# Attention values with v as the stationary operand, and softmax sums spread by a matrix of ones

## The chip, the cores and the metric

The kernel runs on one core of one Trainium2 chip. The metric is the device time of one execution in microseconds (us), lower is better. The profile is of one execution; its engines are PE (TensorE matmuls), PEld (TensorE weight loads), DVE (VectorE), ACT (ScalarE), POOL (GpSimd) and SP (SyncE, here a queue of DMAs).

## What is computed

Eight batches of eight heads, 576 tokens and 64 elements a head. Heads 0 to 3 see a sliding window of 32 tokens, heads 4 to 7 a dilated window: every fourth token, 32 of them. The result goes through a two-layer network with a squared ReLU.

```python
# q, k, v: (8, 8, 576, 64) float32; w_in (512, 2048); w_out (2048, 512)
scores = q @ k.T / sqrt(64)
rel = pos[:, None] - pos[None, :]
mask_plain = (rel >= 0) & (rel < 32)                    # heads 0..3
mask_dil = (rel >= 0) & (rel < 128) & (rel % 4 == 0)    # heads 4..7
attn = softmax(where(mask, scores, -1e9))
x = (attn @ v).transpose(0, 2, 1, 3).reshape(4608, 512)
out = maximum(x @ w_in, 0) ** 2 @ w_out                 # (4608, 512) float32
```

## The kernel before

The order of instructions on each engine is the order in which the program writes them (a manual schedule). Every batch has an attention part; its 576 result rows go, transposed, into `xT` (512 features over 4 x 128 partitions, all 4608 tokens). The network runs over nine chunks of 512 tokens: `mm1_gen` makes 16 tiles `ph` of 128 hidden features by 512 tokens (four matmuls each), ScalarE takes the ReLU (`rt`, L269) and VectorE its square (`g`, L270); `mm2_gen` makes four tiles `po` of 128 tokens by 512 outputs (16 matmuls each), ScalarE copies them out (`ot`, L284) and a DMA stores them (L285, on SP's queue but for chunk 0).

The two are interleaved by hand. A generator yields after every two matmuls of the network, and `pump(n)` issues the next n of these steps, so a step is two 512-column matmuls. A chunk has 64 steps, 32 of `mm1` and 32 of `mm2`; the stores of its four token tiles fall in steps 40, 48, 56 and 64. In the loop over batches 2 to 7, the chunk `b - 1` runs beside batch `b`: 24 steps, then the scores with a gap of 4 steps behind each of four groups, then the values with a gap of 2 behind each of eleven but the last, then what is left. Batch 1 runs beside the second half of chunk 0 (`mm2_by_rows_gen`) with gaps of 1 and 2. Batch 0 has no network work yet; there `fill_gen` puts idle matmuls (`pf`) between its groups.

Attention in a batch, by groups on TensorE:

- Batches 0 and 1 are transposed on TensorE (`t_sliding` into `pt`, `t_dilated` into `pd`, copies by VectorE and ScalarE); later ones come through a DRAM tile and a transposing DMA (`keep_sliding_qk`, `keep_dilated_qk`, `transpose_sliding`, `transpose_dilated`). `after_transposes` makes GpSimd wait for these before it issues the next loads. GpSimd also reorders q and k (`by_token`, `nr`) and casts v (`cast_v`).
- Scores: `s_sliding` (12 matmuls `ps` of 96 columns) and `s_dilated` (16 matmuls `pz` of 72 columns), two of each. They contract over 64 elements, so two heads' matmuls stand in the two halves of the rows. A result tile has keys on the partitions and queries along the free axis. `softmax` takes the exponential on ScalarE (L380) and the product with a 0/1 mask on VectorE (L381) and leaves the weights in `AT`.
- Values: `av_sliding` (three groups `pav`) and `av_dilated` (four groups `paw`). Each has eight matmuls with a 128x128 piece of the weights as the stationary operand and v, with a 65th column of ones, as the moving one. The 65th column of the result is the sum of the weights. `normalize` takes its reciprocal (L423) and multiplies (L424) into `x`, with tokens on the partitions.
- Transposes: `x_sliding` and `x_dilated` turn `x` round (`px`, `py`, two groups each), and ScalarE copies it into `xT` (L473, L491).

The attention groups take their PSUM from `papool`, which has two buffers of two banks, so a group waits until the tile two before it has been read. The network's tiles have four banks of their own (`pmool`).

Of the kernel before, what the change touches and what calls it, by code (L numbers as in the profile page):

```python
# [13 lines left out]
P = 128  # L14
# [3 lines left out]
def kernel(  # L18
# [13 lines left out]
    DIL = 4  # L32
# [27 lines left out]
    xp = ctx.enter_context(tc.tile_pool(name="xp", bufs=4))  # L60
# [19 lines left out]
    AT = const.tile([P, 8, 640], FP16, name="AT")  # L80
    vp = [const.tile([P, NB, HH, D + 2], FP16, name=f"vp{r}") for r in range(2)]
    vd = [const.tile([P, 2, DIL, HH, D + 2], FP16, name=f"vd{r}") for r in range(2)]
# [3 lines left out]
    maskp = const.tile([P, UW], FP16, name="maskp")  # L86
    maskd = const.tile([P, UW], FP16, name="maskd")
# [70 lines left out]
    def cast_sliding_v(b):  # L158
        for m in range(0, NB, 2):
            nc.gpsimd.tensor_copy(vp[b % 2][:, m : m + 2, :, 0:D], sv[:, m : m + 2, :, :])  # L160

    def cast_dilated_v(b):
        for t in range(2):
            for c in range(0, DIL, 2):
                nc.gpsimd.tensor_copy(  # L165
                    vd[b % 2][:, t, c : c + 2, :, 0:D],
                    sd[:, t, :, D * c : D * (c + 2)].rearrange("p h (c d) -> p c h d", d=D),
                )
# [44 lines left out]
    warm = const.tile([P, 1], FP32, name="warm")  # L213
    nc.vector.memset(warm, 0.0)
    nc.scalar.activation(warm, warm, ACTF.Exp)
# [17 lines left out]
    nc.vector.memset(AT[:, :, UW:640], 0.0)  # L233
    for r in range(2):
        nc.vector.memset(QKTp[r][:, 1, :, 0:PADP], 0.0)
        nc.vector.memset(QKTd[r][:, 1, :, 0:KPAD], 0.0)
        nc.vector.memset(vp[r][:, :, :, D : D + 1], 1.0)
        nc.vector.memset(vp[r][0:PADP, 0, :, D : D + 1], 0.0)
        nc.vector.memset(vd[r][:, 1, :, :, D : D + 1], 1.0)
        nc.vector.tensor_scalar(  # L240
            out=vd[r][:, 0, :, :, D],
            in0=relf[:, 0:1].unsqueeze(2).to_broadcast([P, DIL, HH]),
            scalar1=-PADD + 0.5,
            scalar2=None,
            op0=ALU.is_lt,
        )
# [118 lines left out]
    def t_dilated(b, n, a, wide):  # L365
        for w, (s0, s1) in enumerate(((0, 5), (5, 9))):
            p_ = pt(f"pd{b}_{a}_{w}", wide)
            for s in range(s0, s1):
                j = 4 * s + 2 * a
                nc.tensor.transpose(  # L370
                    p_[:, P * (s - s0) : P * (s - s0 + 1)], n[:, D * j : D * (j + 2)], ident
                )
            copy(
                nc.scalar if w else nc.vector,
                QKTd[b % 2][:, :, a, KPAD:].rearrange("x i (c s) -> x i c s", s=9)[:, :, :, s0:s1],
                p_[:, 0 : P * (s1 - s0)].rearrange("x (s i c) -> x i c s", i=2, c=64),
            )

    def softmax(u, ps, mask):
        nc.scalar.activation(AT[:, u, 0:UW], ps[:, :, 0 : UW // 2], ACTF.Exp, scale=scale)  # L380
        nc.vector.tensor_mul(AT[:, u, 0:UW], AT[:, u, 0:UW], mask)  # L381

    def s_sliding(b, hp):
        tiles = [pa(f"ps{b}_{hp}_{half}") for half in range(2)]
        for half, ps in enumerate(tiles):
            for m3 in range(3):
                m = 3 * half + m3
                for e in range(2):
                    r = slice(D * e, D * (e + 1))
                    nc.tensor.matmul(  # L390
                        ps[:, e, QB * m3 : QB * (m3 + 1)],
                        QKTp[b % 2][r, 1, hp, QB * m : QB * m + P],
                        QKTp[b % 2][r, 0, hp, PADP + QB * m : PADP + QB * (m + 1)],
                        start=True,
                        stop=True,
                    )
        for half, ps in enumerate(tiles):
            softmax(2 * hp + half, ps, maskp)
# [20 lines left out]
    def normalize(b, what, pav, w):  # L419
        x = xp.tile([QB, 2, HH, D], FP16, name=f"x{b}_{what}", tag="x")  # L420
        rcp = xp.tile([QB, 2, HH], FP32, name=f"rcp{b}_{what}", tag="rcp")
        pv = pav[0:w, :, 0 : HH * (D + 2)].rearrange("p i (h d) -> p i h d", d=D + 2)
        nc.vector.reciprocal(rcp[0:w], pv[:, :, :, D])  # L423
        nc.vector.tensor_tensor(  # L424
            out=x[0:w],
            in0=pv[:, :, :, 0:D],
            in1=rcp[0:w].unsqueeze(3).to_broadcast([w, 2, HH, D]),
            op=ALU.mult,
        )
        return x  # L430

    def av_sliding(b, mp):
        pav = pa(f"pav{b}_{mp}")
        for i in range(2):
            m = 2 * mp + i
            for h in range(HH):
                off = (h % 2) * 288 + (m % 3) * QB
                nc.tensor.matmul(  # L438
                    pav[:, i, h * (D + 2) : h * (D + 2) + D + 1],
                    AT[:, 2 * (h // 2) + m // 3, off : off + P],  # L440
                    vp[b % 2][:, m, h, 0 : D + 1],
                    start=True,
                    stop=True,
                )
        return normalize(b, f"p{mp}", pav, QB)

    def av_dilated(b, t, a):
        pav = pa(f"paw{b}_{t}_{a}")
        for e in range(2):
            for h in range(HH):  # L450
                off = e * 288 + a * 144 + t * QD
                nc.tensor.matmul(  # L452
                    pav[:, e, h * (D + 2) : h * (D + 2) + D + 1],
                    AT[:, 4 + h, off : off + P],
                    vd[b % 2][:, t, 2 * a + e, h, 0 : D + 1],
                    start=True,
                    stop=True,
                )
        return normalize(b, f"d{t}_{a}", pav, QD)

    def x_sliding(b, half, xs, wide):
        px = pt(f"px{b}_{half}", wide)
        for m3 in range(3):
            m = 3 * half + m3
            x = xs[m // 2][:, m % 2].rearrange("p h d -> p (h d)")
            for c in range(2):
                nc.tensor.transpose(  # L467
                    px[:, 288 * c + QB * m3 : 288 * c + QB * (m3 + 1)],
                    x[:, P * c : P * (c + 1)],
                    ident[0:QB, 0:QB],  # L470
                )
        t0 = b * S + 288 * half
        nc.scalar.copy(  # L473
            xT[:, 0:2, t0 : t0 + 288],
            px[:, 0:UW].rearrange("x (c t) -> x c t", c=2),
        )

    def x_dilated(b, t, xs, wide):
        py = pt(f"py{b}_{t}", wide)
        for a in range(2):  # L480
            for e in range(2):
                x = xs[a][:, e].rearrange("p h d -> p (h d)")
                for c in range(2):
                    o = 288 * c + QD * (2 * a + e)
                    nc.tensor.transpose(  # L485
                        py[:, o : o + QD],
                        x[0:QD, P * c : P * (c + 1)],
                        ident[0:QD, 0:QD],
                    )
        t0 = b * S + 288 * t  # L490
        nc.scalar.copy(  # L491
            xT[:, 2:4, t0 : t0 + 288].rearrange("x c (i r) -> x c i r", r=DIL),
            py[:, 0:UW].rearrange("x (c r i) -> x c i r", c=2, r=DIL),
        )

    def attn_scores(b, gap, less=0):
        for hp in range(2):
            s_sliding(b, hp)
            pump(gap)
        for g in range(2):  # L500
            s_dilated(b, g)
            pump(gap - g * less)

    def attn_values(b, gap, wide=False):
        xs = []
        for mp in range(3):
            xs.append(av_sliding(b, mp))
            pump(gap)
        x_sliding(b, 0, xs, wide)
        pump(gap)  # L510
        ys = [av_dilated(b, 0, 0)]
        pump(gap)
        x_sliding(b, 1, xs, wide)
        pump(gap)
        ys.append(av_dilated(b, 0, 1))
        pump(gap)
        zs = []
        for a in range(2):
            zs.append(av_dilated(b, 1, a))
            pump(gap)  # L520
        x_dilated(b, 0, ys, wide)
        pump(gap)
        x_dilated(b, 1, zs, wide)
# [12 lines left out]
    pending.append(fill_gen())  # L536
    for hp in range(2):
        s_sliding(0, hp)
        pump(1)
    for a in range(2):  # L540
        t_dilated(0, m, a, False)
    pump(2)
    for g in range(2):
        s_dilated(0, g)
        pump(1)
    load_w_out((0, 1))
# [11 lines left out]
    attn_values(0, 1)  # L558
# [7 lines left out]
    pump(7)  # L566
    n, m = nsd[1]
    for hp in range(2):
        t_sliding(1, n, hp, True)
        pump(1)  # L570
    for a in range(2):
        t_dilated(1, m, a, True)
        pump(1)
    attn_scores(1, 2, 1)
    attn_values(1, 1, True)
# [7 lines left out]
    for b in range(2, B):  # L583
# [11 lines left out]
        pump(24)  # L595
        attn_scores(b, 4)
        if not last:
            dp = keep_sliding_qk(b + 1, nr)
        attn_values(b, 2)
# [37 lines left out]
```

The softmax here doesn't subtract the row's maximum and nothing guards it: scores larger than these inputs give would overflow.

## Time and profile before

| | us |
|---|---|
| three runs | 321.22, 321.86, 323.31; median 321.86 |
| the profiled execution | 320.36 |
| its span, first to last instruction | 318.3 |
| matmuls po and ph, 576 of 512 columns each | 140.8 and 128.3 busy |
| matmuls paw (256) and pav (192), 65 columns | 13.3 and 10.0 busy |
| matmuls ps (192) and pz (256) | 7.5 and 7.2 busy |
| transposes py (128) and px (96) | 6.9 and 6.7 busy |

Busy time is a union of intervals; the duration of one pipelined matmul (379 ns for 512 columns, 193 ns for 65) is longer than the distance to the next. What a group costs TensorE is therefore read from the starts of its neighbours. In the lists of instruction groups, "out<-in" are tiles by the program's names, L numbers are lines, and the last figures are busy us, the mean ns of one, and the engine's idle time before.

### The profile page before, as it was taken

What the parts mean: (1) busy time and instruction counts of PE and PEld (TensorE: products, weight loads), DVE (VectorE), ACT (ScalarE), POOL (GpSimd) and SP (SyncE); (2) the same over time, 40 slices, a digit from 0 to 9 for tenths busy, and PEclk for the clock granted to TensorE, in tenths of its full rate; (3) what the DMA queues carried; (4) which work ended last, traced back from release to release, by engine and by line L of the source; (5) the groups of instructions that cost most, each with busy time, mean ns of one, the idle gap of its engine ahead of it and who ended that gap; (6) DMA issues with size and microseconds to landing.
All of it is one profiled execution on the core that took longest, in us unless ns stands there. A gap on an engine that the chain in (4) does not pass through costs nothing.

```text
span 318.3 us, 6260 instructions
## 1 busy us (share of the span) xinstructions
PE 302.9 (95%) x2484; PEld 157.8 (50%) x2484; DVE 162.2 (51%) x353; ACT 168.7 (53%) x286; POOL 79.2 (25%) x119
## 2 busy tenths in 40 slices
PE   1899989999999999999999999999999999999995
PEld 1455544454555445545555455555554555445542
DVE  5683548447543674369435952596256525203400
ACT  2726635568436834684368536762577256316611
POOL 4192018403480361137012800371000000000000
PEclk9999999999999999999999999999999999999999
DMA  7999998999999993998399839984810110010011
GB/s 126 197 155 215 207 210 144 195 257 192 211 259 224 205 270 100 217 194 184 106 205 184 191 91 216 191 172 126 173 44 1 68 68 0 27 72 36 1 66 66
DMA packets 79213, 46.67 MB, mean 147 GB/s; under 512 B 54352, under 2 KB 72784, under 8 KB 79184
## 3 DMA queue, kind: packets, MB, share of 16 engines
q1 hardware_dynamic: 64928, 31.60, 40.8%
q0 software_dynamic: 14256, 14.68, 28.1%
q8 instruction: 19, 0.31, 0.4%
q14 instruction: 10, 0.08, 0.1%
HBM read 39.85 MB, written 16.52 MB: 177 GB/s over the span
## 4 chain that ended last, share of the span: by engine, by line
PE 68%; DMA 12%; DVE 7%; SPq 5%; POOL 3%; issue 2%; ACT 2%; POOLq 0%; ACTq 0%
PE ph L259 31%; PE po L274 31%; SPq L120 4%; DMA wi<-in_moe_w_in_dram 4%; DVE AT L381 3%; DMA sd<-in_v_dram 2%; PE paw L452 2%; DMA sv<-in_v_dram 2%; DMA ns<-in_q_dram 2%; DVE g L270 1%; DMA out_dram<-ot 1%; PE ps L390 1%; PE pav L438 1%; DMA QKTp<-dp 1%; PE py L485 1%
## 5 line engine op out<-in xcount | busy, mean ns | idle before, releaser
L274 PE MATMUL po<-wo,g 128*128 128x512 f16 x576 | 140.8, 379 | 0.0
L259 PE MATMUL ph<-xT,wi 128*128 128x512 f16 x576 | 128.3, 380 | 0.3 <-ACT xT L491 0.3
L270 DVE TENSOR_TENSOR g<-rt 128x512 f16<-128x512 f16 x144 | 66.2, 462 | 98.5 <-ACT rt L269 98.0
L269 ACT ACTIVATE rt<-ph 128x512 f16<-128x512 f32 x144 | 85.9, 599 | 31.4 <-PE ph L259 31.0
L259 PEld LDWEIGHTS <-wi 128*128 128x128 f16 x576 | 64.1, 113 | 58.1 <-issue 0.7
L274 PEld LDWEIGHTS <-g 128*128 128x128 f16 x576 | 49.7, 97 | 46.3
L284 ACT COPY ot<-po 128x512 f32<-128x512 f32 x36 | 21.1, 587 | 54.0 <-PE po L274 51.4
L473 ACT COPY xT<-px 128x576 f16<-128x576 f16 x16 | 10.2, 639 | 31.8 <-PE px L467 31.8
L160 POOL CAST vp<-sv 128x512 f16<-128x512 f32 x24 | 16.5, 712 | 32.9 <-DMA sv<-in_v_dram 32.9
L381 DVE TENSOR_TENSOR AT<-AT,maskd 128x576 f16<-128x576 f16 x32 | 20.3, 664 | 5.3 <-ACT AT L380 4.4
L424 DVE TENSOR_TENSOR x_d<-paw,rcp_d 72x512 f16<-72x512 f32 x32 | 22.0, 687 | 1.1
L380 ACT ACTIVATE AT<-pz 128x576 f16<-128x576 f32 x32 | 18.9, 650 | 5.7 <-PE pz L409 5.6
L165 POOL CAST vd<-sd 128x512 f16<-128x512 f32 x32 | 20.9, 691 | 4.2 <-DMA sd<-in_v_dram 3.6
L381 DVE TENSOR_TENSOR AT<-AT,maskp 128x576 f16<-128x576 f16 x32 | 18.0, 568 | 5.1 <-ACT AT L380 2.8
L380 ACT ACTIVATE AT<-ps 128x576 f16<-128x576 f32 x32 | 19.0, 650 | 1.1 <-PE ps L390 1.0
L111 POOL COPY nr<-ns 128x2304 f16<-128x2304 f16 x6 | 13.0, 2161 | 25.6 <-DMA ns<-in_q_dram 25.6
L204 POOL COPY seen<-QKTp 128x1 f16<-128x1 f16 x5 | 1.3, 267 | 63.0 <-DMA QKTp<-dp 63.0
L424 DVE TENSOR_TENSOR x_p<-pav,rcp_p 96x512 f16<-96x512 f32 x24 | 16.5, 687 | 0.8
L423 DVE RECIPROCAL rcp_d<-paw 72x8 f32<-72x8 f32 x32 | 6.5, 202 | 19.5 <-PE paw L452 19.5
L452 PEld LDWEIGHTS <-AT 128*128 128x128 f16 x256 | 12.1, 98 | 8.5 <-PE px L467 1.0
L491 ACT COPY xT<-py 128x576 f16<-128x576 f16 x16 | 10.2, 640 | 10.7 <-PE py L485 10.5
L452 PE MATMUL paw<-vd,AT 128*128 128x65 f16 x256 | 13.3, 193 | 0.1
(58 smaller groups left out, 143.2 us busy)
## 6 DMA issues: line engine op xcount, KB each, us to landing
out_dram<-ot SPq DMA_DIRECT2D x32, 256.0 KB, 2.2
sv<-in_v_dram SPq DMA_DIRECT2D x40, 128.0 KB, 5.3
sd<-in_v_dram SPq DMA_DIRECT2D x8, 512.0 KB, 10.9
dp<-nr SPq DMA_DIRECT2D x12, 288.0 KB, 4.3
ns<-in_k_dram POOLq DMA_DIRECT2D x8, 288.0 KB, 6.0
ns<-in_q_dram POOLq DMA_DIRECT2D x8, 288.0 KB, 7.4
sd<-in_v_dram SPq DMA_DIRECT2D x8, 288.0 KB
wo<-in_moe_w_out_dram POOLq DMA_DIRECT2D x4, 512.0 KB, 12.9
```

The lines of the kernel that those rows point to most:

```text
L111: nc.gpsimd.tensor_copy(r.rearrange("x j h d -> x h j d"), n.rearrange("x h (j d) -> x h j d", d=D))
L160: nc.gpsimd.tensor_copy(vp[b % 2][:, m : m + 2, :, 0:D], sv[:, m : m + 2, :, :])
L165: nc.gpsimd.tensor_copy(vd[b % 2][:, t, c : c + 2, :, 0:D], sd[:, t, :, D * c : D * (c + 2)].rearrange("p h (c d) -> p c h d", d=D),)
L259: nc.tensor.matmul(ph, wi4[ffc // 4][:, dmk, :, ffc % 4], xs[:, dmk, :], start=(dmk == 0), stop=(dmk == NDM - 1),)
L269: nc.scalar.activation(rt, ph[:], ACTF.Relu)
L270: nc.vector.tensor_mul(g[:, ffc, :], rt, rt)
L274: nc.tensor.matmul(po, g[:, ffc, t * P : (t + 1) * P], wo[ffc // 4][:, ffc % 4, :], start=(ffc == 0), stop=(ffc == NFF - 1),)
L284: nc.scalar.copy(ot, po)
L380: nc.scalar.activation(AT[:, u, 0:UW], ps[:, :, 0 : UW // 2], ACTF.Exp, scale=scale)
L381: nc.vector.tensor_mul(AT[:, u, 0:UW], AT[:, u, 0:UW], mask)
L424: nc.vector.tensor_tensor(out=x[0:w], in0=pv[:, :, :, 0:D], in1=rcp[0:w].unsqueeze(3).to_broadcast([w, 2, HH, D]), op=ALU.mult,)
L452: nc.tensor.matmul(pav[:, e, h * (D + 2) : h * (D + 2) + D + 1], AT[:, 4 + h, off : off + P], vd[b % 2][:, t, 2 * a + e, h, 0 : D + 1], st ...
```

## The change

The values are computed transposed. `v` (128 tokens by 64 elements, without the column of ones) is the stationary operand and the masked weights are the moving one, so a matmul gives 64 elements by 96 or 72 queries. Two heads fill the upper and lower half of the partitions of one PSUM tile, in the layout of `xT`; the transposes and their copies go.

The sums come from matmuls of their own: `ones` (128x64) is stationary, the weights move in pieces of 288 columns, and each sum stands in all 64 partitions of its head (`st`). `shares` takes the logarithm of these on ScalarE and the exponential of its negative, which is the inverse (`r`, 128 x 576 float32). VectorE multiplies `u` by `r` into `xT`.

Padded keys, until now kept out of the sums by zeros in the column of ones, are kept out by masks: `maskp0` for the first half of the sliding heads, and zeros in `maskd`. One activation table with both functions is loaded by name. The order changes too: `attn_scores` holds the four `shares` groups between and behind the scores with one gap for all, `attn_values` has four groups in place of eleven, the loop pumps 22, then gaps of 3 and 3, and in batch 0 all copies of `t_dilated` are VectorE's.

```diff
-        nc.vector.reciprocal(rcp[0:w], pv[:, :, :, D])
-        nc.vector.tensor_tensor(
-            out=x[0:w],
-            in0=pv[:, :, :, 0:D],
-            in1=rcp[0:w].unsqueeze(3).to_broadcast([w, 2, HH, D]),
-            op=ALU.mult,
+    HW = UW // 2
+
+    def shares(b, what, weights):
+        st = pa(f"st{b}_{what}")
+        for h in range(HH):
+            e = slice(D * (h % 2), D * (h % 2 + 1))
+            nc.tensor.matmul(st[e, h // 2, 0:HW], ones, weights(h), start=True, stop=True)
+        r = rp.tile([P, 2, HW], FP32, name=f"r{b}_{what}", tag="r")
+        nc.scalar.activation(r, st[:, :, 0:HW], ACTF.Ln)
+        nc.scalar.activation(r, r, ACTF.Exp, scale=-1.0)
+        return r
...
+    def av_sliding(b, half, r):
+        u = pa(f"up{b}_{half}")
+        for m3 in range(3):
             for h in range(HH):
-                off = (h % 2) * 288 + (m % 3) * QB
+                e = slice(D * (h % 2), D * (h % 2 + 1))
+                off = HW * (h % 2) + QB * m3
                 nc.tensor.matmul(
-                    pav[:, i, h * (D + 2) : h * (D + 2) + D + 1],
-                    AT[:, 2 * (h // 2) + m // 3, off : off + P],
-                    vp[b % 2][:, m, h, 0 : D + 1],
+                    u[e, h // 2, QB * m3 : QB * (m3 + 1)],
+                    vp[b % 2][:, 3 * half + m3, h, :],
+                    AT[:, 2 * (h // 2) + half, off : off + QB],
...
+        nc.vector.tensor_mul(xT[:, 0:2, t0 : t0 + HW], u[:, :, 0:HW], r)
+
+    def av_dilated(b, t, r):
+        u = pa(f"ud{b}_{t}")
+        for c in range(DIL):
             for h in range(HH):
...
+                    u[e, h // 2, QD * c : QD * (c + 1)],
+                    vd[b % 2][:, t, c, h, :],
+                    by_class(h, t)[:, c // 2, c % 2],
...
+    def attn_scores(b, gap):
+        rs = []
         for hp in range(2):
             s_sliding(b, hp)
             pump(gap)
+        for half in range(2):
+            rs.append(shares_sliding(b, half))
+            pump(gap)
         for g in range(2):
             s_dilated(b, g)
-            pump(gap - g * less)
...
+        for t in range(2):
+            rs.append(shares_dilated(b, t))
             pump(gap)
+        return rs
+
+    def attn_values(b, rs, gap):
+        for half in range(2):
+            av_sliding(b, half, rs[half])
+            pump(gap)
+        for t in range(2):
+            av_dilated(b, t, rs[2 + t])
+            if t == 0:
+                pump(gap)
...
-    pump(7)
+    pump(4)
     n, m = nsd[1]
     for hp in range(2):
         t_sliding(1, n, hp, True)
-        pump(1)
+        pump(3)
     for a in range(2):
         t_dilated(1, m, a, True)
-        pump(1)
-    attn_scores(1, 2, 1)
-    attn_values(1, 1, True)
+        pump(2)
+    rs = attn_scores(1, 1)
+    pump(2)
+    attn_values(1, rs, 1)
...
-        pump(24)
-        attn_scores(b, 4)
+        pump(22)
+        rs = attn_scores(b, 3)
         if not last:
             dp = keep_sliding_qk(b + 1, nr)
-        attn_values(b, 2)
+        attn_values(b, rs, 3)
```

More of the change, by code (lines that the diff above doesn't have):

```diff
@@ L59 @@
     natp = ctx.enter_context(tc.tile_pool(name="natp", bufs=4))
-    xp = ctx.enter_context(tc.tile_pool(name="xp", bufs=4))
+    rp = ctx.enter_context(tc.tile_pool(name="rp", bufs=4))
     gp = ctx.enter_context(tc.tile_pool(name="gp", bufs=2))
@@ L79 @@
     QKTd = [const.tile([P, 2, 2, KPAD + S], FP16, name=f"QKTd{r}") for r in range(2)]
-    AT = const.tile([P, 8, 640], FP16, name="AT")
-    vp = [const.tile([P, NB, HH, D + 2], FP16, name=f"vp{r}") for r in range(2)]
-    vd = [const.tile([P, 2, DIL, HH, D + 2], FP16, name=f"vd{r}") for r in range(2)]
+    AT = const.tile([P, 8, UW], FP16, name="AT")
+    vp = [const.tile([P, NB, HH, D], FP16, name=f"vp{r}") for r in range(2)]
+    vd = [const.tile([P, 2, DIL, HH, D], FP16, name=f"vd{r}") for r in range(2)]
+    ones = const.tile([P, D], FP16, name="ones")
     sv = stg.tile([P, NB, HH, D], FP32, name="sv")
@@ L86 @@
     maskp = const.tile([P, UW], FP16, name="maskp")
+    maskp0 = const.tile([P, UW], FP16, name="maskp0")
     maskd = const.tile([P, UW], FP16, name="maskd")
@@ L159, in cast_sliding_v @@
         for m in range(0, NB, 2):
-            nc.gpsimd.tensor_copy(vp[b % 2][:, m : m + 2, :, 0:D], sv[:, m : m + 2, :, :])
+            nc.gpsimd.tensor_copy(vp[b % 2][:, m : m + 2], sv[:, m : m + 2, :, :])
     def cast_dilated_v(b):
@@ L165, in cast_dilated_v @@
                 nc.gpsimd.tensor_copy(
-                    vd[b % 2][:, t, c : c + 2, :, 0:D],
+                    vd[b % 2][:, t, c : c + 2],
                     sd[:, t, :, D * c : D * (c + 2)].rearrange("p h (c d) -> p c h d", d=D),
@@ L212 @@
     make_identity(nc, ident)
-    warm = const.tile([P, 1], FP32, name="warm")
-    nc.vector.memset(warm, 0.0)
-    nc.scalar.activation(warm, warm, ACTF.Exp)
+    nc.scalar.preload_act_table_set("natural_log_exp_and_others")
     relf = const.tile([P, QB], FP32, name="relf")
@@ L232 @@
         )
-    nc.vector.memset(AT[:, :, UW:640], 0.0)
+    nc.vector.tensor_copy(maskp0, maskp)
+    nc.vector.memset(maskp0.rearrange("p (e m w) -> p e m w", e=2, m=3)[0:PADP, :, 0], 0.0)
+    nc.vector.memset(maskd.rearrange("p (n t w) -> p n t w", t=2, w=QD)[0:PADD, :, 0], 0.0)
+    nc.vector.memset(ones, 1.0)
     for r in range(2):
@@ L236 @@
         nc.vector.memset(QKTd[r][:, 1, :, 0:KPAD], 0.0)
[L237 to L246, printed above, removed]
     wi4 = []
@@ L363, in t_sliding, with t_dilated @@
             )
-    def t_dilated(b, n, a, wide):
+    def t_dilated(b, n, a, wide, both=False):
         for w, (s0, s1) in enumerate(((0, 5), (5, 9))):
@@ L373, in t_dilated @@
             copy(
-                nc.scalar if w else nc.vector,
+                nc.scalar if w and not both else nc.vector,
                 QKTd[b % 2][:, :, a, KPAD:].rearrange("x i (c s) -> x i c s", s=9)[:, :, :, s0:s1],
@@ L379, in softmax @@
     def softmax(u, ps, mask):
-        nc.scalar.activation(AT[:, u, 0:UW], ps[:, :, 0 : UW // 2], ACTF.Exp, scale=scale)
-        nc.vector.tensor_mul(AT[:, u, 0:UW], AT[:, u, 0:UW], mask)
+        nc.scalar.activation(AT[:, u], ps[:, :, 0 : UW // 2], ACTF.Exp, scale=scale)
+        nc.vector.tensor_mul(AT[:, u], AT[:, u], mask)
     def s_sliding(b, hp):
@@ L397, in s_sliding @@
         for half, ps in enumerate(tiles):
-            softmax(2 * hp + half, ps, maskp)
+            softmax(2 * hp + half, ps, maskp if half else maskp0)
     def s_dilated(b, g):
@@ L417, in s_dilated, with shares_sliding, by_class, shares_dilated @@
             softmax(4 + 2 * g + h, ps, maskd)
[L419 to L423, printed above, removed]
-        nc.vector.tensor_tensor(
-            out=x[0:w],
-            in0=pv[:, :, :, 0:D],
-            in1=rcp[0:w].unsqueeze(3).to_broadcast([w, 2, HH, D]),
-            op=ALU.mult,
-        )
[L430 to L435, printed above, removed]
+    HW = UW // 2
[8 more added lines that the diff above has]
+        return r
+    def shares_sliding(b, half):
+        return shares(
+            b, f"p{half}", lambda h: AT[:, 2 * (h // 2) + half, HW * (h % 2) : HW * (h % 2 + 1)]
+        )
+    def by_class(h, t):
+        return AT[:, 4 + h].rearrange("p (e a t w) -> p t a e w", e=2, a=2, t=2)[:, t]
+    def shares_dilated(b, t):
+        return shares(b, f"d{t}", lambda h: by_class(h, t))
+    def av_sliding(b, half, r):
+        u = pa(f"up{b}_{half}")
+        for m3 in range(3):
             for h in range(HH):
-                off = (h % 2) * 288 + (m % 3) * QB
+                e = slice(D * (h % 2), D * (h % 2 + 1))
+                off = HW * (h % 2) + QB * m3
                 nc.tensor.matmul(
-                    pav[:, i, h * (D + 2) : h * (D + 2) + D + 1],
-                    AT[:, 2 * (h // 2) + m // 3, off : off + P],
-                    vp[b % 2][:, m, h, 0 : D + 1],
+                    u[e, h // 2, QB * m3 : QB * (m3 + 1)],
+                    vp[b % 2][:, 3 * half + m3, h, :],
+                    AT[:, 2 * (h // 2) + half, off : off + QB],
                     start=True,
@@ L444, in av_sliding @@
                 )
[L445 to L449, printed above, removed]
+        t0 = b * S + HW * half
+        nc.vector.tensor_mul(xT[:, 0:2, t0 : t0 + HW], u[:, :, 0:HW], r)
+    def av_dilated(b, t, r):
+        u = pa(f"ud{b}_{t}")
+        for c in range(DIL):
             for h in range(HH):
-                off = e * 288 + a * 144 + t * QD
+                e = slice(D * (h % 2), D * (h % 2 + 1))
                 nc.tensor.matmul(
-                    pav[:, e, h * (D + 2) : h * (D + 2) + D + 1],
-                    AT[:, 4 + h, off : off + P],
-                    vd[b % 2][:, t, 2 * a + e, h, 0 : D + 1],
+                    u[e, h // 2, QD * c : QD * (c + 1)],
+                    vd[b % 2][:, t, c, h, :],
+                    by_class(h, t)[:, c // 2, c % 2],
                     start=True,
@@ L458, in av_dilated @@
                 )
[L459 to L475, printed above, removed]
-        )
[L478 to L496, printed above, removed]
+        t0 = b * S + HW * t
+        nc.vector.tensor_mul(
+            xT[:, 2:4, t0 : t0 + HW].rearrange("x c (i r) -> x c i r", r=DIL),
+            u[:, :, 0:HW].rearrange("x c (r i) -> x c i r", r=DIL),
+            r.rearrange("x c (r i) -> x c i r", r=DIL),
+        )
+    def attn_scores(b, gap):
+        rs = []
         for hp in range(2):
@@ L499, in attn_scores @@
             pump(gap)
+        for half in range(2):
+            rs.append(shares_sliding(b, half))
+            pump(gap)
         for g in range(2):
             s_dilated(b, g)
-            pump(gap - g * less)
[L504 to L507, printed above, removed]
-            pump(gap)
[L509 to L519, printed above, removed]
-            pump(gap)
-        x_dilated(b, 0, ys, wide)
-        pump(gap)
-        x_dilated(b, 1, zs, wide)
+            pump(gap)
+        for t in range(2):
+            rs.append(shares_dilated(b, t))
+            pump(gap)
+        return rs
[7 more added lines that the diff above has]
+                pump(gap)
     n, m = nsd[0]
@@ L536 @@
     pending.append(fill_gen())
+    rs = []
     for hp in range(2):
@@ L540 @@
     for a in range(2):
-        t_dilated(0, m, a, False)
-    pump(2)
+        t_dilated(0, m, a, False, True)
+    pump(1)
+    rs.append(shares_sliding(0, 0))
+    pump(1)
     for g in range(2):
@@ L545 @@
         pump(1)
+    rs.append(shares_sliding(0, 1))
+    pump(2)
     load_w_out((0, 1))
@@ L557 @@
     nr = by_token(2, ns)
-    attn_values(0, 1)
+    for half in range(2):
+        av_sliding(0, half, rs[half])
+        pump(1)
+    for t in range(2):
+        rs.append(shares_dilated(0, t))
+        pump(1)
+    for t in range(2):
+        av_dilated(0, t, rs[2 + t])
+        pump(2)
     pending.clear()
@@ L569 @@
         t_sliding(1, n, hp, True)
-        pump(1)
+        pump(3)
     for a in range(2):
         t_dilated(1, m, a, True)
-        pump(1)
-    attn_scores(1, 2, 1)
-    attn_values(1, 1, True)
+        pump(2)
+    rs = attn_scores(1, 1)
+    pump(2)
+    attn_values(1, rs, 1)
     pump(1000)
```

## The prediction, made before the change was run

> **What bounds the kernel now.** I read the engine table and the slices first, then the waits of TensorE, then the last batch's chain, then narrow timeline windows at the edges of attention groups.
>
> The page: busy us and share of the span by engine; then the granted clock in tenths.
>
> ```profile
> PE 302.9 (95%) x2484; PEld 157.8 (50%) x2484; DVE 162.2 (51%) x353; ACT 168.7 (53%) x286; POOL 79.2 (25%) x119
> PEclk9999999999999999999999999999999999999999
> ```
>
> TensorE is full from slice 2 to the end, at full clock. The list of waits confirms it: these are its largest after start-up.
>
> ```profile
> PE pav L438 <- DVE rcp_p L423: 2.0, 5, 0.5
> PE ps L390 <- DMA QKTp<-dp: 0.2, 1, 0.2
> ```
>
> So TensorE's own work sets the time, and attention counts by what it costs TensorE. The chain in the last batch prices a group (start, duration, what):
>
> ```profile
> 243.78 0.37 PE pz L409 x16
> 244.15 1.83 PE po L274 x8
> 245.98 0.26 PE pav L438 x8
> 246.23 0.86 PE po L274 x4
> ...
> 249.33 0.26 PE px L467 x6
> ```
>
> Four 512-column matmuls take 0.86, so 0.216 each (2.4 columns a ns). A group of values or of transposes adds 0.26. The score groups, where 64 of 128 rows are used, are dearer than 0.37: the eight matmuls behind take 1.83, not 1.73. The timeline (start, duration) shows why:
>
> ```profile
> 138.26 0.59 PE L259 MATMUL ph<-xT,wi 128*128 128x512 f16 x2
> 138.78 0.43 PE L390 MATMUL ps<-QKTp 64*128 64x96 f16 x12
> 139.15 0.62 PE L259 MATMUL ph<-xT,wi 128*128 128x512 f16 x2
> ...
> 146.86 0.81 PE L274 MATMUL po<-wo,g 128*128 128x512 f16 x3
> 147.51 0.42 PE L438 MATMUL pav<-vp,AT 128*128 128x65 f16 x8
> 147.76 0.59 PE L274 MATMUL po<-wo,g 128*128 128x512 f16 x2
> ...
> 41.68 0.48 PE L353 MATMUL pt<-ident,ns 64*64 64x64 f16 x36
> 42.09 0.39 PE L274 MATMUL po<-wo,g 128*128 128x512 f16 x1
> ```
>
> From the first of two matmuls to the scores is 0.52, where two pitches are 0.43: 0.09 lost on entry; leaving loses another 0.09. Full-array pav shows neither: three pitches from 146.86 make 147.51. In the median over the score groups of batches 1 to 7 a group costs 0.46 (six pairs of 96 columns at 0.0425 make 0.255), so a switch in and out costs 0.20. The pt window shows 64x64 tiles overlapping fourfold: 36 matmuls of 64 columns in 0.41 with its exit.
>
> **What the Trainium skill says.** "TensorEngine Tiling (Array Packing)", Key Properties: "Changing tiling mode (not just tile) drains the TensorE", and different tiles run in parallel. The trace agrees for row-split (0.09 + 0.09) and 64x64 work; it has no 128-row, 64-column matmul. "SBUF — State Buffer", Terms: VectorE and GpSimd share a port pair, and the loser blocks for the whole instruction. The trace agrees (nr, below). "ScalarE: Activation LUTs", Table sets: ln and exp share natural_log_exp_and_others, and a switch to another set costs about 2.7 us. The trace has one load, of 1.28 us.
>
> **The change part by part.** Per batch on TensorE:
> - Removed: 24 + 32 matmuls of 65 columns in seven groups and 28 transposes in four: 11 x 0.257 = 2.83.
> - Added, sums by ones: four groups, each two pairs of 288 columns. A pair streams in 0.122 (288 / 2.4, plus 0.0025) if its two 64-column tiles overlap: 0.245.
> - Added, values: two groups of six pairs of 96 columns (0.255), two of eight pairs of 72 (8 x 0.032 = 0.26).
> - Streaming: 4 x 0.245 + 2 x 0.255 + 2 x 0.26 = 2.01. Every one of the eight new groups lies between full-array matmuls, so each switches in and out. Bounds for that: 0 (all 128 rows stay in use) and 0.20. I take 0.20, as pt also pays it: 1.63.
> - Balance: 3.64 - 2.83 = +0.81 a batch. Batches 1 to 7: +5.7. Without switches it is -0.82, so -5.7.
>
> If the pairs don't overlap, streaming doubles: +2.0 a batch.
>
> VectorE: seven reciprocals (0.20) and seven 0.687 products go, four products of 576 columns come (0.687 x 576 / 512 = 0.77): 6.2 - 3.1 = 3.1 less a batch. It was hidden except for pav's 2.0 above, which falls away. ScalarE: four copies of 0.64 go, four Ln and four Exp of 128x576 come (about 0.65 each, the score exponential's row): +2.6 a batch. On average hidden, but it lands inside the scores stage.
>
> Late masks. The ones matmul needs the masked weights soon after the scores; before, only pav did, much later. One undisturbed batch, from the first score matmul (t = 0), gap of 3 steps = 1.30, with durations of the rows (exponential 0.65, following 0.54 later; relu 0.60; mask 0.46): second scores 1.78 to 2.2; their exponentials 2.2 to 2.85 and 2.74 to 3.4; first mask 3.35; shares of half 0 are due at 3.56, so fit. Ln and Exp for them run 4.3 to 5.65, for half 1 6.1 to 7.45 (st's buffer is then free for pz). Dilated scores 7.05, then about 8.85 (pa buffers free at 8.5 and 9.05); their exponentials end 10.05 and 10.6, masks 10.55 and 11.1. Dilated shares come due at 10.65 and stop at the fourth head until 11.15: 0.35 to 0.4 lost. Behind it stand TensorE's dense matmuls, so the loss is whole. Six batches: 2.4.
>
> GpSimd's copy nr makes it worse:
>
> ```profile
> 141.56 2.11 POOL L111 COPY nr<-ns 128x2304 f16<-128x2304 f16 x1 [4.79 <-DMA ns<-in_q_dram]
> 141.73 2.22 DVE L270 TENSOR_TENSOR g<-rt 128x512 f16<-128x512 f16 x1 [0.21 <-ACT rt L269]
> ...
> 143.87 1.64 DVE L381 TENSOR_TENSOR AT<-AT,maskp 128x576 f16<-128x576 f16 x2
> ```
>
> A 0.42 product takes 2.22, then masks take 0.82 under the casts of v. In batches 4 to 6 it comes 2.8 to 4.3 us after the first scores. In the change the transposes on SP's queue stand behind the store of token tile 1, not 2 (pumps end at 55 of 64, not 60), some 4.5 us earlier in the stream, less what the later stage start gives; so nr moves to about -1.2 to +0.3. It then ends before or among the sliding masks; the casts behind it slow them to 0.82. Bounds per batch: 0 (a clear miss) and 2.6 (nr on the first mask). I take 0.9 for each of these three: 2.7. Stalls are then 5.1, against 2.0 in batches 2 to 7 before: +3.1.
>
> Batch 1 has gaps of one step (0.43) in the scores, so nearly every mask and every pa buffer comes late: by the same walk 4.3 lost, against 3.5 before, where one third was in pt and pd, which now get 2 to 3 steps. +0.8.
>
> Batch 0: TensorE fills idle time there. All four pd copies go to VectorE (4 x 0.8 from 12.3, so the dilated scores start near 15.5, not 14.03), but the transposes and their copies go; walking the queues, xT is whole near 25.4, not 25.14. +0.3. Moving masks, ones and memsets costs nothing: they hide under the wait for ns. The smaller tiles (no 66th column) change no transfer. The first table load stays one.
>
> Sum: 5.7 + 3.1 + 0.8 + 0.3 = 9.9. The profiled execution took 320.36 (span 318.3 and 2.1 around it): 330.3. The median of the three runs is 321.86, 1.5 higher; on it the sum gives 331.8. I predict 331.
>
> **Rivals.**
> 1. No switch cost (the other side). A column split keeps all rows busy, so entering and leaving need not empty the array: place, the edges of the eight groups; price, 56 x 0.20 = 11.4. The point where it decides is 0.10 a group, half of the row-split's price: there the TensorE balance is nil. At zero the sum is -5.7 + 4.2 = -1.5, 320.4; if the stalls are covered too (masks early, pav's 2.0 gone) 314 to 316. For it: no trace line shows this shape. Against: pt, which is also column-split, pays on exit. Chance 0.21, of which 0.08 is clearly faster.
> 2. Pairs don't overlap. 128-row tiles of 64 columns run one after the other: +14, so 345. For it: pairs here read different moving operands over the same rows, while pt reads the identity. Against: pt's four at once. 0.07.
> 3. Ln and Exp fall into different table sets. Eight switches a batch at 1.28 or more keep ScalarE busy 10 us longer a batch, in a stage where it is full: over 380. Against: the set is named in the change, and the skill says it holds both. 0.04.
>
> **How the numbers follow.** The forecast has 0.68, its own range 326 to 338. The range 320 to 341 leaves out the fastest 0.08 and most of rivals 2 and 3 (0.11). A measurement of this kernel tells about 1% from no change: 318.6 to 325.1. Slower: nearly all of the forecast and rivals 2 and 3, 0.78; same, 0.13, rival 1 with stalls; faster 0.09.
>
> **What would show it.** Right: st and u groups that lose about 0.09 before and after; st groups of four near 0.45; waits of TensorE's st on the mask (DVE AT) of about 5 us in all, worst where nr runs; no pav wait; one table load; mm1's first matmul near 25.4. Wrong: a pitch of 0.216 into and out of the new groups (rival 1), 0.12 between neighbouring heads' sums (rival 2), more table loads (rival 3), or masks long done when st comes. If TensorE's idle time falls below the old one, the stall term is wrong and the time goes to about 326.

## The result, and the profile after

The changed kernel takes 340.64 us (median of four runs, 336.63 to 343.12), the kernel before 321.69 beside it: 1.050 times as long, interval 1.040 to 1.059. The prediction was 331 with a range of 320 to 341, so the sign holds, the range holds by 0.4 us, and the size is short by 9.6 us. The ratio, like every difference of times below, is taken from executions within 1.5% of the fastest of their kernel, which are 336.63 and 339.25 here (mean 337.9). The profiled execution took 342.03 (span 339.9), so what follows accounts for one that is about 4 us longer than those two.

The page after shows the engines, then the granted clock.

```profile
PE 314.5 (93%) x2388; PEld 147.9 (44%) x2388; DVE 149.3 (44%) x269; ACT 186.0 (55%) x315; POOL 79.6 (23%) x119
PEclk9999999999999979999999999999999999999999
```

TensorE has fewer instructions (2388, not 2484), yet is busy 11.6 us longer, and its share falls by two points: there is both more work and more waiting. ScalarE got 17 us heavier, as foreseen (2.6 a batch). VectorE got only 13 us lighter, about half of the 3.1 a batch that were foreseen: the dilated product takes 1.13 us where 0.77 was assumed, and masks and squares are stretched more, to 4.5 us more in all. One slice of the clock is not full. TensorE's waits:

```profile
PE st_p L418 <- DVE AT L374: 6.6, 7, 1.7
PE st_d L418 <- DVE AT L374: 3.4, 2, 3.1
PE ph L252 <- ACT ot L277: 2.8, 1, 2.8
PE pz L402 <- ACT AT L373: 1.3, 4, 0.4
```

The sums groups wait for masks, 10.0 us in all; pav's waits are gone with its groups; a wait for the output tile `ot` is new. The chain in batch 7, where GpSimd is idle, prices the new groups (start, duration, what):

```profile
269.35 0.37 PE st_d L418 x4
269.72 1.40 PE po L267 x6
271.12 0.38 PE up L441 x12
271.49 1.40 PE po L267 x6
...
274.67 0.38 PE ud L456 x16
275.05 1.40 PE po L267 x6
```

Six network matmuls behind a new group take 1.40 where six pitches of 0.216 are 1.30. So each new group pays on leaving, as the scores do. Measured from the last network matmul ahead to the first behind, less one pitch, an undisturbed st group costs 0.461, up 0.471, ud 0.476. These costs hold the streaming and the price of one visit, that is of leaving the full array for the half-width groups and coming back. Four neighbours of 288 columns in 0.461 also show that two heads' half-width matmuls overlap: four in a row would need about 0.48 at 2.4 columns a ns, without any switch.

Where the 21.6 us between the two spans arise follows from the start of each chunk's last matmul. Beside batches 2 to 7, another 0.1 a batch lies in the starts of network matmuls:

| | before | after | difference | what it holds |
|---|---|---|---|---|
| to the end of chunk 0 (batches 0, 1) | 62.59 | 64.47 | +1.88 | batch 0: 0.98 later into the network; batch 1: TensorE 0.91, waits 3.45 against 3.48 |
| beside batch 2 | 32.73 | 39.74 | +7.01 | TensorE 0.91, mask 3.38, `ot` 2.97, less 0.4 of old pav waits |
| beside batch 3 | 32.79 | 37.05 | +4.26 | TensorE 0.91, masks 2.1, half clock 1.6, less 0.4 of old pav waits |
| beside batches 4, 5, 6 | 98.31 | 105.62 | +7.31 | TensorE 2.7, masks 5.4, less 1.2 of old pav waits |
| beside batch 7 | 32.37 | 33.56 | +1.19 | TensorE 0.91, mask 0.16 |

The last two chunks take the same 55.25. Three readings carry this. First, the masks: VectorE, then GpSimd, then TensorE in batch 2, then VectorE and GpSimd in batch 3, from timeline windows (start, duration).

```profile
87.17 4.21 DVE L374 TENSOR_TENSOR AT<-AT,maskd 128x576 f16<-128x576 f16 x2 [0.52 <-ACT AT L373]
...
88.92 2.12 POOL L113 COPY nr<-ns 128x2304 f16<-128x2304 f16 x1
...
91.44 0.28 PE L418 MATMUL st_d<-AT,ones 128*64 128x288 f16 x1 [3.10 <-DVE AT L374]
...
115.30 2.74 DVE L374 TENSOR_TENSOR AT<-AT,maskp 128x576 f16<-128x576 f16 x2
...
115.51 2.21 POOL L113 COPY nr<-ns 128x2304 f16<-128x2304 f16 x1 [5.66 <-DMA ns<-in_q_dram]
```

In batch 2 two masks that take 0.46 each when undisturbed end at 91.38, just after nr; the fourth head's sum and everything behind it on TensorE stand for 3.10. In batch 3 nr covers the second of the first two masks. In batches 4 and 5 nr starts 0.56 and 0.29 after the first score matmul, in batch 6 it starts 0.16 before it; in all three it stretches a square of VectorE to 1.9 to 2.4, and the masks stand behind that.

Second, the store. The waits of ScalarE and TensorE around 64 us:

```profile
69.61 0.59 ACT L277 COPY ot<-po 128x512 f32<-128x512 f32 x1 [5.00 <-DMA out_dram<-ot]
...
62.20 0.57 POOL L278 DMA_DIRECT2D out_dram<-ot  x1 [1.96 <-ACT ot L277]
...
61.64 4.27 SPq L200 DMA_TRANSPOSE QKTd<-dd  x2
...
70.25 1.02 PE L252 MATMUL ph<-xT,wi 128*128 128x512 f16 x4 [2.81 <-ACT ot L277]
```

Chunk 0's first store is issued 0.56 after the transposing DMAs start; before, it came 1.5 ahead of them. It lands at 69.51, 7.3 after its issue (4.3 before). The fourth output copy needs that buffer, and the next chunk's `ph` needs the PSUM that the copy frees. This is in part chance: in the trace of e4 (below), whose program is the same up to there, the store is issued at 60.70, 1.15 ahead of the transposing DMAs, lands after 4.8, and `ph` waits 0.3.

Third, the dip in the clock, from the windows view (start:end, length, busy us of PE, PEld, DVE, ACT and POOL with counts, granted clock, then DMA share and GB/s):

```profile
119.50:123.50 4.00, 3.88 (x14) 1.25 (x14) 2.39 (x5) 2.57 (x4) 3.24 (x5) 0.61 0.29 95
```

TensorE runs at half clock for 3.41 us from 120.35, just after the stall of 1.7 us for the masks of batch 3. Network matmuls then start 0.43 apart instead of 0.216. The late starts add up to 1.1, and a sums group in that stretch costs 0.97 instead of 0.46 though its masks were done at 120.34, so the interval costs about 1.6.

### The profile page after: what moved, and what is told of

The parts are those of the page before. It is cut to its first block, busy times and chain, and to the rows that moved or that the text cites. A ratio compares the mean times of both kernels' runs of the same rounds, so it can differ in the third digit from the quotient of the medians.

```text
span 339.9 us, 6006 instructions
## 1 busy us (share of the span) xinstructions
PE 314.5 (93%) x2388; PEld 147.9 (44%) x2388; DVE 149.3 (44%) x269; ACT 186.0 (55%) x315; POOL 79.6 (23%) x119
## 4 chain that ended last, share of the span: by engine, by line
PE 82%; DVE 8%; ACT 4%; DMA 4%; issue 2%; POOL 0%; ACTq 0%; POOLq 0%
PE po L267 36%; PE ph L252 34%; DVE AT L374 5%; DVE g L263 3%; PE pf L317 2%; DMA out_dram<-ot 2%; PE st_d L418 2%; ACT AT L373 2%; PE st_p L418 2%; PE ud L456 2%; PE up L441 2%; DMA ns<-in_q_dram 1%; PE pz L402 1%; PE pd L363 1%; PE ps L383 1%
## 5 line engine op out<-in xcount | busy, mean ns | idle before, releaser
L267 PE MATMUL po<-wo,g 128*128 128x512 f16 x576 | 137.0, 380 | 0.0
L252 PE MATMUL ph<-xT,wi 128*128 128x512 f16 x576 | 131.8, 383 | 2.8 <-ACT ot L277 2.8
L263 DVE TENSOR_TENSOR g<-rt 128x512 f16<-128x512 f16 x144 | 69.5, 486 | 106.6 <-ACT rt L262 106.2
L449 DVE TENSOR_TENSOR xT<-up,r_p 128x576 f16<-128x576 f32 x16 | 12.1, 758 | 33.4 <-PE up L441 33.4
L464 DVE TENSOR_TENSOR xT<-ud,r_d 128x576 f16<-128x576 f32 x16 | 18.1, 1134 | 12.9 <-PE ud L456 12.9
L420 ACT ACTIVATE r_p<-st_p 128x576 f32<-128x576 f32 x16 | 10.5, 659 | 11.1 <-PE st_p L418 11.1
L420 ACT ACTIVATE r_d<-st_d 128x576 f32<-128x576 f32 x16 | 10.4, 649 | 8.3 <-PE st_d L418 8.3
L418 PEld LDWEIGHTS <-ones 128*64 128x64 f16 x128 | 5.3, 109 | 22.0 <-issue 16.8
L418 PE MATMUL st_p<-AT,ones 128*64 128x288 f16 x64 | 8.3, 315 | 6.6 <-DVE AT L374 6.6
L418 PE MATMUL st_d<-AT,ones 128*64 128x288 f16 x64 | 8.5, 298 | 3.4 <-DVE AT L374 3.4
```

The source lines that it names most:

```text
L252: nc.tensor.matmul(ph, wi4[ffc // 4][:, dmk, :, ffc % 4], xs[:, dmk, :], start=(dmk == 0), stop=(dmk == NDM - 1),)
L263: nc.vector.tensor_mul(g[:, ffc, :], rt, rt)
L267: nc.tensor.matmul(po, g[:, ffc, t * P : (t + 1) * P], wo[ffc // 4][:, ffc % 4, :], start=(ffc == 0), stop=(ffc == NFF - 1),)
L418: nc.tensor.matmul(st[e, h // 2, 0:HW], ones, weights(h), start=True, stop=True)
L420: nc.scalar.activation(r, st[:, :, 0:HW], ACTF.Ln)
L464: nc.vector.tensor_mul(xT[:, 2:4, t0 : t0 + HW].rearrange("x c (i r) -> x c i r", r=DIL), u[:, :, 0:HW].rearrange("x c (r i) -> x c i r", ...
```

## The experiments

**e1: sums and value groups in pairs.** This separates the price of a visit from the price of the matmuls.

```diff
         for half in range(2):
             rs.append(shares_sliding(b, half))
-            pump(gap)
+        pump(2 * gap)
```
The same for the dilated sums, and for the two sliding and the two dilated value groups.

> The changed kernel with the two sums groups of the sliding heads side by side on TensorE, likewise the two of the dilated heads, the two sliding and the two dilated value groups; the gaps between are put behind the pair. Theory (a switch between the full array and half-width tiles costs TensorE 0.20 us in and out together, per visit): 8 visits a batch become 4, so 28 visits fewer in batches 1 to 7, about 5.6 us less TensorE time; a pair of sums groups should then add about 0.72 to the stream instead of 2 x 0.46. The second group of a pair comes 1.3 us earlier, so up to 2 us of that may come back as waits for masks: 3.5 to 5.6 us faster than the changed kernel. Rival (the half-width matmuls themselves are slow, no price of the visit): a pair adds 0.92 as before, no gain. Rival (ScalarE's logarithm and exponential are what is late): no gain or slower, since they bunch.

Measured: 339.1 us in the median (three executions of 339.1 to 339.4, one of 328.24 of which there is no trace). The time settles nothing, but the price of a group does. TensorE's timeline in batch 7:

```profile
264.54 0.68 PE L418 MATMUL st_d<-AT,ones 128*64 128x288 f16 x8
265.15 2.76 PE L267 MATMUL po<-wo,g 128*128 128x512 f16 x12
267.85 0.70 PE L441 MATMUL up<-AT,vp 128*64 128x96 f16 x24
268.48 2.76 PE L267 MATMUL po<-wo,g 128*128 128x512 f16 x12
271.17 0.71 PE L456 MATMUL ud<-AT,vd 128*64 128x72 f16 x32
```

A pair of sums adds 0.706 where two single ones add 0.922; a pair of up 0.727 (0.942), of ud 0.737 (0.952). Twice the matmuls for one visit save 0.215 each time: that is the price of a visit, 0.01 to 0.02 above the one taken. The rival of slow matmuls is out. In the profile st_p waits 7.9 us for masks, more than in the changed kernel (6.6), and there are two half-clock intervals, so in this execution the gain was given back. That the second sums of a pair come earlier and meet the same late masks fits this.

**e2: four `ot` buffers.** `ot` gets a pool of its own with four buffers in place of three.

> The changed kernel with four buffers instead of three for the output tile ot. Theory: the 2.97 us in which TensorE waits at 67 us for ScalarE, which waits for a free ot whose store landed 7.3 us after its issue, is gone: 3.0 us faster than the changed kernel, the wait of ph for ot absent from TensorE's list. Rival (DMAs are what bound batches 1 to 3): the wait moves to the transposed q and k of batch 2, and under 1 us is gained.

Measured: 334.48, 1.036 times the kernel before (1.032 to 1.040) and 3.9 less than the changed kernel, close to the 3.0 of the theory. The wait for `ot` is gone from TensorE's list, whose longest rows after start-up are now:

```profile
PE st_p L419 <- DVE AT L375: 4.4, 4, 1.6
...
PE st_d L419 <- DVE AT L375: 0.5, 2, 0.3
```

In the profiles the span fell by 8.8, since the half-clock interval and the 3.1 wait of batch 2's st_d are gone too: nr now starts at 87.87, 1.4 after the group that needs the last mask has gone on. The same copy of 2.1 us cost 3.4 or next to nothing, by where it fell. No wait for the transposed q and k stands in the list, so the rival, that DMAs were the bound, is out.

**e3: nr left out.** q and k go to DRAM as they were loaded, so what this kernel leaves out is the reordering of tokens in batches 2 to 7; all else is computed. (The DMA behind it reads the tile in its new form.)

```diff
-        r = natp.tile([P, 9, HH, D], FP16, name=f"nr{b}", tag="n")
-        nc.gpsimd.tensor_copy(
-            r.rearrange("x j h d -> x h j d"), n.rearrange("x h (j d) -> x h j d", d=D)
-        )
-        return r
+        return n
```

> The changed kernel without GpSimd's copy nr: q and k of batches 2 to 7 go to the DRAM tile in the order in which they were loaded, so their tokens are out of order; everything else is computed. Theory (VectorE's masks stand still while GpSimd copies): the waits of the sums groups for masks in batches 2 to 6 (3.4, 2.4, 1.6, 1.7, 1.6 us in the profile of the changed kernel) fall to under 0.3 each, and the half-clock interval at 120 us goes with the stall before it: 8 to 11 us faster than the changed kernel. Rival (ScalarE is late, not VectorE): the waits stay above 1 us a batch, at most 2 us faster. The copies of v into 16 bit stay and may still slow masks.

Measured: 330.5, 7.5 less, 1.025 (1.022 to 1.028), just short of the 8 to 11 expected. The chunks beside batches 3 to 7 take 33.56 each (one 33.66), just what batch 7 takes in the changed kernel. The casts of v stay, so in these batches it was nr that held the masks, not ScalarE. One long wait for masks is left:

```profile
PE st_p L414 <- DVE AT L370: 2.3, 1, 2.3
```

It lies in batch 1, where a mask runs from 48.59 to 51.42, beside a DMA issue of GpSimd and four casts of v without a break behind it. The half-clock interval at 120 us is gone, but one of 6.83 us stands in batch 1.

**e4: nr and the casts of v held back until the last mask.** Everything is computed.

```diff
-            nr = by_token(b + 1, ns)
-            cast_v(b + 1)
         pump(22)
         rs = attn_scores(b, 3)
         if not last:
+            nc.gpsimd.tensor_copy(seen, AT[:, 7, 0:1])
+            nr = by_token(b + 1, ns)
+            cast_v(b + 1)
             dp = keep_sliding_qk(b + 1, nr)
```

> The changed kernel, in batches 2 to 6 with GpSimd's copy nr and its casts of v for the next batch held back until the last mask of the running batch is done (a one-element copy of that mask's output on GpSimd stands ahead of them). Theory: as without nr, the waits for masks fall to 0.2 to 0.4 a batch; the transposing DMAs start some 3 us later than in the changed kernel, about where they did before the change, and are not waited for: 8 to 11 us faster than the changed kernel. If the later DMAs are waited for, a wait of ps on QKTp shows and takes part of it back: 4 to 7. Rival (ScalarE is late): at most 2 us.

Measured: 328.59, 9.4 less, 1.020 (1.017 to 1.024), within the 8 to 11 of the theory. TensorE's largest waits after start-up:

```profile
PE ps L383 <- DMA QKTp<-dp: 1.1, 1, 1.1
PE pz L402 <- ACT AT L373: 0.9, 3, 0.4
...
PE st_d L418 <- DVE AT L374: 0.3, 1, 0.3
```

The masks are hardly waited for any more, and the later DMAs cost 1.1 once, in batch 2. No half-clock interval is left while TensorE works. The `ot` wait is 0.3 here without four buffers, so e2's gain is not all additional. The chunks beside batches 3 to 7 take 33.56 each again: this is the change with masks on time (0.16 of mask waits a batch is left), and it still loses about 1.2 us a batch to the undisturbed 32.37 of before.

**e5: the kernel before, with nr and the casts held back as in e4.**

> The kernel before, with nothing of the change, but nr and the casts of v held back until the last mask of the running batch is done, as in e4. Theory (late masks cost the kernel before only the 2.0 us of pav's waits, as its values come long after the masks): 0 to 2 us faster than the kernel before, pav's waits for rcp under 0.5 us in all; so what e4 gained is a weakness of the change, not of both. Rival (GpSimd's copies cost both kernels about the same): 6 to 10 us faster than before.

Measured: 319.67 against 321.75, 0.995 (0.993 to 0.997). Two rows of TensorE's waits:

```profile
PE ps L390 <- DMA QKTp<-dp: 1.2, 1, 1.2
...
PE pav L438 <- DVE rcp_p L423: 0.6, 2, 0.4
```

pav's waits for rcp fall from 2.0 to 0.6 us, and ps waits 1.2 for QKTp in batch 2. So holding GpSimd's copies back gains about 2 us in the kernel before and about 9 in the changed one.

**e6: pairs, four `ot` buffers, nr and the casts held back; one step more ahead of each pair of sums, one less behind.**

> The changed kernel with e1 (sums and value groups in pairs), e2 (four ot buffers) and e4 (nr and casts held back) together, and one step of each gap behind a pair of sums moved ahead of it, so that the second masks are done. Theory (visits, late masks and the late store are the three costs, and they add): e4's 328.6 less 28 x 0.2 of visits and under 1 us of batch 1: 321 to 324, level with the kernel before, since the TensorE balance is then 2.88 against 2.83 a batch. Rival (each removed wait is replaced by another): 326 to 330.

Measured: 324.58, 1.007 (1.004 to 1.010), at the upper edge of the theory's range. The pairs cost 0.706, as in e1, but the dilated scores now wait for ScalarE, 3.1 us in all. The two rows of these waits, then the chain at one pair:

```profile
PE pz L403 <- ACT AT L374: 2.3, 9, 0.4
...
PE pz L403 <- ACT r_p L421: 0.8, 1, 0.8
...
212.59 0.39 PE st_p L419 x4
...
212.99 0.66 ACT r_p L421
...
213.68 0.68 ACT r_p L422
214.36 0.55 ACT r_p L421
...
217.72 0.31 PE pz L403 x8
```

ScalarE's order is logarithm, inverse, logarithm, inverse. The PSUM of the second sums is freed only by the third of these, and pz and the relus stand behind it.

**e7: e4 with one reciprocal on VectorE in place of logarithm and exponential.**

```diff
-        nc.scalar.activation(r, st[:, :, 0:HW], ACTF.Ln)
-        nc.scalar.activation(r, r, ACTF.Exp, scale=-1.0)
+        nc.vector.reciprocal(r, st[:, :, 0:HW])
```

> e4 with the inverse by one reciprocal on VectorE, reading the sums from PSUM, in place of logarithm and exponential on ScalarE. ScalarE loses 8 x 0.65 us a batch, VectorE gains 4 x 0.8 or so. Theory (the inverse lies off the path once masks are on time, whoever makes it): within 1 us of e4. Rival (ScalarE's fullness in the scores stage is what is left): 2 to 4 us faster than e4, the remaining waits of pz for ScalarE gone. A third possibility: the reciprocal delays masks in VectorE's queue, and the waits of the sums groups for masks come back: 2 us or more slower than e4.

Measured: 393.13, 1.222 (1.216 to 1.227). Only the sign of the third possibility came true, and not through its waits: up and pz wait for r, and no sums group waits for masks among TensorE's largest waits. The longest of these waits, and the row of the reciprocals (busy, mean ns of one, idle before):

```profile
PE up L440 <- DVE r_d L420: 16.9, 13, 2.3
...
L420 DVE RECIPROCAL r_p<-st_p 128x576 f32<-128x576 f32 x16 | 59.8, 3742 | 0.0
```

I had taken 0.8 us, as for a product. It is 3.74, or 6.5 ns an element. Before the change the 8 elements a partition took 0.20, which hid this. With the sums spread over all elements, the two passes on ScalarE (0.65 and 0.68 us) are the cheap way. The granted clock averaged 0.94 in this execution, so part of the loss is half clock; the theory, that it does not matter who makes the inverse, was not tested at equal cost.

**e8: e6 with both logarithms of a pair ahead of both inverses.**

> e6 with ScalarE's order changed in a pair of sums: both logarithms first, which free the PSUM tiles of the sums, then both inverses. In e6 every dilated score group waits about 0.4 us for ScalarE. Theory (what is left in e6 is ScalarE's turn behind the sums; the inverse itself is not yet needed): pz's waits fall from 3.1 us in all to under 1.5, and a batch from 32.89 to about 32.5 us, 1 to 2.5 us faster than e6. Rival (ScalarE is simply full in this stage, whatever its order): the waits move from one pz group to the next, within 0.5 us of e6.

Measured: 321.58, 2.6 less than e6, 0.999 (0.997 to 1.001) against the kernel before, so there is no difference from that. The row of pz's waits for ScalarE:

```profile
PE pz L403 <- ACT AT L374: 1.3, 3, 0.8
```

They fall from 3.1 to 1.3, and a chunk takes 32.60 us where e6 took 32.89. Most of e6's excess was ScalarE's order, not its load.

**e9: e5 with four `ot` buffers.**

> e5 (the kernel before with nr and the casts held back) with four ot buffers. Theory (the late store was a wait of the changed kernel alone; before, ScalarE waited 2.1 us for ot, but TensorE did not): within 0.7 us of e5. Rival (the store is near the path there too): 1 us or more faster than e5.

Measured: 319.64, 0.994 (0.992 to 0.997), the same as e5. In the kernel before, a fourth buffer gains nothing, so the late store is no cost there. e5 and e9 beat both kernels, by half a per cent and without anything of the change.

## Why the prediction was right in sign and short in size

1. TensorE's balance, +0.81 a batch, was right in kind; 0.91 was measured (3.74 of new groups, not 3.64). Each of the eight visits pays about 0.215, and half-width pairs overlap. e1 shows both, and rivals 1 and 2 fall. Another 0.1 a batch is in network matmuls that start some 0.027 late behind a visit beside `mm1`. Together this is about 7 us instead of 5.7. The Trainium skill ("TensorEngine Tiling (Array Packing)", Key Properties) states that a change of tiling mode drains TensorE; the runs agree, with 0.215 for a split of the columns alone. They show the price, not the draining itself.
2. One activation table was right. The trace after has one load, of 1.28 us, as before, so rival 3 is out.
3. Masks without GpSimd: 0.35 to 0.4 a batch was predicted, 0.16 measured in batch 7. The walk through the queues was good to a quarter of a microsecond.
4. Masks under nr is the term that was sized most wrongly. I put nr at -1.2 to +0.3 from the first scores and took 0.9 for each of batches 4 to 6. It came at -0.16 to +0.56, hardly later, and cost 1.6 to 1.75, so the price was wrong more than the place. Batches 2 and 3, where I took no disturbance and gave no reason, lost 3.4 and 2.1. All mask waits of batches 2 to 7 come to about 11 where the sum had 5.1. The bound of 2.6, named for batches 4 to 6, was exceeded in batch 2. e3 and e4 show that nr is the cause, in agreement with the shared ports of "SBUF — State Buffer", Terms, in the Trainium skill: a mask or square that starts while nr runs takes 1.8 to 2.4 in all but one of 16 cases in the traces (all but e7's), instead of 0.42 to 0.46. e4 against e5 shows that the change made it matter.
5. Batch 1: +0.8 was predicted, and the waits were equal in fact. But the order of DMAs at its end, which I did not walk, gave the 2.97 wait for `ot` in the profiled execution. I had priced the SP queue's transposes only as a cause for nr, not as a neighbour of GpSimd's stores.
6. Batch 0: +0.3 was predicted, +0.98 measured. The dilated product into `xT` takes 1.13, not 0.77, but that explains little. The last product into `xT` ends at 26.10, while in e3 and e4, whose batch 0 is the same, it ends at 25.15 and 25.32, near the predicted 25.4. Most of the 0.98 belongs to this execution; why it came so late is open.
7. The half-clock interval (1.6 us) was not foreseen.

In the profiled execution 7.1 for TensorE, 9.1 for masks net of the old 2.0, 3.0 for `ot`, 1.6 for the clock and 1.0 for batch 0 come to 21.8, against the 21.6 of the spans. What the prediction called the wrong case (masks long done) did not occur.

That the range held is partly luck. Its upper end lies 0.4 us above the median, two of the four executions lie beyond it, and terms missed in both directions: batch 1 and the undisturbed masks cost less than foreseen, while the masks under nr, the store and the clock cost more.

## What to carry to other kernels

Fewer instructions and columns on the bounding engine are no gain if each group now enters and leaves a split of the array: price the visit (here about 0.215 us), count the visits, and put groups of the same split side by side. When a consumer moves from long after a result to right behind it, look at everything that can hold the producer, GpSimd's copies for VectorE above all; holding back the same copies was worth about 2 us before and 9 after. An operation that is cheap on 8 elements a partition need not be so on 576.

## What the runs showed that was not expected

VectorE's reciprocal takes 6.5 ns an element (3.74 us for 576 a partition), against about 1.15 ns for each of the two ScalarE passes.

A mask that started at 87.91 in the changed kernel, while GpSimd issued two DMAs, stood still for a whole microsecond before nr began at 88.92, and on to 91.38. In e3 another, started during a DMA issue, stood until 51.42 through four casts, though elsewhere a mask beside casts mostly takes 0.8 to 0.9. Both began during such an issue, but so did some 195 other masks and squares in the traces (e7's left out), and only three of those stood for over 2 us. What sets these few apart is open.

Half-clock intervals of 3.41 to 10.24 us stand among TensorE's work in the traces of the changed kernel, e1, e3 and e7, and in none of the others. Each begins during a stall of TensorE of 1.3 to 4.2 us or within 2 us behind it. But the stalls of 2.81 and 3.10 in the changed kernel and of 1.76 in e6 have none behind them, so a stall of that length is not enough by itself; what decides was not tried.
